# Skip term of the first slab moved from TensorE to VectorE, with a new instruction order on VectorE and a new order of the last output matmuls

## Chip, cores and metric

The kernel runs on one core of a Trainium2 chip. The metric is the device time of one execution in microseconds (us); the median of several runs is compared. Engine names are those of the profile: PE is TensorE, PEld its weight loads, DVE VectorE, ACT ScalarE, POOL GpSimd, SP the queue from which nearly all DMAs are issued.

## What is computed

The input x is 2048 x 512 in bf16. Each row is normalised to xn. From xn come two branches whose product is added to x:

```
xn  = layernorm(x)
Bu  = xn @ B_bar^T                       # complex, 512 states
h_t = Lam_bar * h_(t-1) + Bu_t           # scan over the 2048 rows
s   = 2 * Re(h @ C^T) + xn * Dskip       # Dskip: the skip term
g   = silu((gelu(xn @ w_gate) * (xn @ w_up)) @ w_down)      # inner width 1376
out = x + s * g
```

## The kernel before

The 2048 rows are four slabs (s = 0 to 3) of 512 rows, and a slab is four groups (m = 0 to 3) of 128 rows. All of x stays in SBUF in one tile, `x_tok`, with 16 groups of 512 columns. A slab goes through these steps:

- **Norm.** VectorE (slabs 0 to 2) or ScalarE (`ln_act`, L548, slab 3) sums the statistics; `ln_out` (L573) lets ScalarE write xn, lets a DMA transpose it into `xnT`, and, where `skip` is called, lets VectorE write z = xn * Dskip (L571), so that the skip term can be added later.
- **FFN.** For j = 0 to 10, `ffn` (L451) makes a gate and an up tile of 512 rows x 128 inner columns (`gu_mm`, L223, eight matmuls); ScalarE evicts both (L463, L464), and VectorE multiplies them into `at`, two j at a time (L469; the last, odd one at L467).
- **Scan.** `u_pair` (L365) makes Bu for half of the states (h = 0 or 1), and `chain` (L402) queues VectorE's work on it: rotate in two products (`pp`, `qq`, L391) and two sums into `Wt` (L395), four scans (L421), four tiny carries (L438 to L441), rotate back in the same way into `hst`.
- **Down.** `down` (L471) makes the FFN output of a group with 11 matmuls; ScalarE takes its silu into `g2` (L481).
- **y.** `y_mm` (L484) makes a group's s with eight matmuls from `hst` and C (L491). Where no z exists (slab 0, and groups 2 and 3 of slab 3), four more matmuls of 128x128 against diagonal matrices of Dskip add the skip term on TensorE (L496). `epi` (L503) is VectorE's end: `yt` = y + z where z exists (L512), `yg` = y * g2 (L513), `ot` = yg + x (L514), then the store. `y_halves` (L519) does the last group in two halves.

Around slab s + 1's FFN the y of slab s are made: `Y_AT` (L360) names the four j after which y_mm of group 0 to 3 stands in TensorE's order. After the FFN of a slab stand the two `u_pair` of the next slab and then the four `down`. In the end (L656 to L664) y of group 0 stands ahead of the four `down` of slab 3, and the other three y behind them.

The order on VectorE is set by a small planner when the program is built. `clk` holds a time for PE and for DVE; `dve(ready, cost, f)` (L348) places an instruction now, after it has let waiting ones go that fit ahead of it by their costs, and `later` (L353) puts scan work on the waiting list; `flush` (L340) empties it up to a named chain, which `y_mm` does ahead of its matmuls. The costs are constants in the text (1.15 for a product, 1.19 for a scan, 0.95 or 1.6 for `epi`). On the chip each engine then runs its own list in that order, and waits where a semaphore says so.

At the start x and the gate and up weights are loaded on SP; the weights come in three pieces of columns (`CUTS`, L93). The x of slab 3 is loaded by `load_x(3)` (L633) during slab 0. xn has four buffers, `ot` two, z nine.

Of the kernel before, what the change touches and what calls it, by code (L numbers as in the profile page):

```python
# [11 lines left out]
ALU = mybir.AluOpType  # L12
# [7 lines left out]
def kernel(  # L20
# [69 lines left out]
        nc.sync.dma_start(out=x_tok[:, a:b, :], in_=x_r[:, a:b, :])  # L90
    for i, v in enumerate((A_log_dt, A_Lambda_im, A_Lambda_re, A_Dskip)):
        nc.scalar.dma_start(out=pv[4 * i : 4 * i + 4, :], in_=v.rearrange("(k p) -> k p", p=P))
    CUTS = (0, 3 * P, 8 * P, F)  # L93

    def load_gu(i):
        a, b = CUTS[i], CUTS[i + 1]
        nc.sync.dma_start(out=wg[:, :, a:b], in_=wg_r[:, :, a:b])
        nc.sync.dma_start(out=wu[:, :, a:b], in_=wu_r[:, :, a:b])

    def load_x(s):  # L100
        nc.sync.dma_start(out=x_tok[:, s * M : (s + 1) * M, :], in_=x_r[:, s * M : (s + 1) * M, :])
# [6 lines left out]
    load_gu(0)  # L108
    load_x(1)
    load_gu(1)  # L110
    load_x(2)
    nc.sync.dma_start(out=Db[:], in_=A_Dskip.unsqueeze(0).to_broadcast([P, D]))
    for h in range(2):
        for ri, src in enumerate((A_B_re, A_B_im)):
            for pt in (h * H2, h * H2 + 1):
                nc.sync.dma_start_transpose(
                    out=BT[:, ri, :, pt * P : (pt + 1) * P], in_=src[pt * P : (pt + 1) * P, :]
                )
    load_gu(2)


    warm = work.tile([P, TS], BF16, name="warm", tag="yg")
# [33 lines left out]
    def bn(s, m):  # L156
        nc.vector.bn_stats(out=st[:, s, m, :], in_=x_tok[:, s * M + m, :])
# [41 lines left out]
        else:  # L199
            eng.tensor_copy(out=o, in_=tp[:, k0:k1, :])  # L200

    bn(0, 0)
    bn(0, 1)
    bn_end(0, 0)
    bn_end(0, 1)
    rstd(0, 0, 2)
# [30 lines left out]
    for j in range(SPLIT):  # L237
        for up in range(2):
            early[j, up] = gu_mm(0, j, up, 0, TS // 2)
        if j == 0:  # L240
            tps += [t_xn0(2, xs[2]), t_xn0(3, xs[3])]
            xnT_out(nc.scalar, 3, tps[3])
    STT(out=thn[:], in0=lim, scalar=1.0 / (2.0 * math.pi), in1=dt_[:], op0=ALU.mult, op1=ALU.mult)
    TT(out=a1[:], in0=lre, in1=dt_[:], op=ALU.mult)
    nc.gpsimd.tensor_tensor(out=rho[:], in0=euler[:], in1=a1[:], op=ALU.pow)
# [111 lines left out]
    ini = {}  # L357
    U_BUFS = 3
    U0_AT = (5, 7)
    Y_AT = {1: (5, 7, 9, 10), 2: (1, 2, 3, 4), 3: (2, 4, 6, 8)}  # L360

    def ca_wide():
        ACT(out=v4(ca[:]), in_=ch[:, :, NB : NB + NA].unsqueeze(3).to_broadcast(W4), func=AF.Copy)  # L363
# [19 lines left out]
    def rotate(dst, src, h, ops, ready, key):  # L383
        hs = slice(h * H2, (h + 1) * H2)
        W = [P, 2, H2, TS]
        box = {}

        def mul(key, tab):
            def f():
                box[key] = work.tile(W, BF16, name=key, tag=key, bufs=1)  # L390
                TT(out=box[key][:], in0=src()[:], in1=tab[:, hs, :].unsqueeze(1).to_broadcast(W), op=ALU.mult)  # L391
            return f

        def comb(i, op):
            return lambda: TT(out=dst()[i], in0=box["pp"][:, i, :, :], in1=box["qq"][:, 1 - i, :, :], op=op)  # L395

        later(ready, 1.15, mul("pp", cos_b), key)
        later(ready, 1.15, mul("qq", sin_b), key)
        for i in range(2):
            later(ready, 0.6, comb(i, ops[i]), key)  # L400

    def chain(s, h, U, hst):  # L402
        hs = slice(h * H2, (h + 1) * H2)
        ready = now() + 0.9
        box = {}

        def wt():
            box["W"] = work.tile([P, 2, H2, TS], BF16, name="Wt", tag="Wt", bufs=1)
            return [box["W"][:, i, :, :] for i in range(2)]

        def wt_dst():
            return wt() if "W" not in box else [box["W"][:, i, :, :] for i in range(2)]

        rotate(wt_dst, lambda: U, h, (ALU.add, ALU.subtract), ready, ("u", s, h))

        def scan(q, ri):
            def f():
                if "F" not in box:
                    box["F"] = work.tile([P, 2, H2, TS], BF16, name="Ft", tag="Ft", bufs=1)
                pt = h * H2 + q  # L420
                nc.vector.tensor_tensor_scan(  # L421
                    out=box["F"][:, ri, q, :], data0=rho[:, pt : pt + 1].to_broadcast([P, TS]),
                    data1=box["W"][:, ri, q, :], initial=0.0 if s == 0 else ini[h][:, ri, q : q + 1],
                    op0=ALU.mult, op1=ALU.add,
                )
            return f

        for q in range(H2):
            for ri in range(2):
                later(ready, 1.19, scan(q, ri))  # L430

        def carry():
            fl = box["F"][:, :, :, TS - 1]
            W = [P, 2, H2]
            ta = work.tile(W, FP32, name="ta", tag="ta")
            tb = work.tile(W, FP32, name="tb", tag="tb")
            it = work.tile(W, FP32, name="it", tag=f"it{h}")
            TT(out=ta[:], in0=fl, in1=cS[:, hs].unsqueeze(1).to_broadcast(W), op=ALU.mult)  # L438
            TT(out=tb[:], in0=fl, in1=sS[:, hs].unsqueeze(1).to_broadcast(W), op=ALU.mult)
            TT(out=it[:, 0, :], in0=ta[:, 0, :], in1=tb[:, 1, :], op=ALU.subtract)  # L440
            TT(out=it[:, 1, :], in0=ta[:, 1, :], in1=tb[:, 0, :], op=ALU.add)  # L441
            ini[h] = it

        if s < NS - 1:
            later(ready, 0.5, carry)
        rotate(
            lambda: [hst[:, i, hs, :] for i in range(2)], lambda: box["F"], h, (ALU.subtract, ALU.add), ready,
            ("h", s, h),
        )

    def ffn(s, j, at):  # L451
        fs = min(P, F - j * P)
        if s == 0 and j < SPLIT:
            g_ps, u_ps = (gu_mm(s, j, up, TS // 2, TS, early[j, up]) for up in range(2))
        else:
            g_ps, u_ps = gu_mm(s, j, 0), gu_mm(s, j, 1)
        pe_takes(2 * KT)
        i = j % 2
        if i == 0:
            pair["g"] = work.tile([P, 2, TS], BF16, name="gt", tag="gt", bufs=3)  # L460
            pair["u"] = work.tile([P, 2, TS], BF16, name="ub", tag="ub", bufs=3)
        gt, ub = pair["g"], pair["u"]
        ACT(out=gt[:fs, i, :], in_=g_ps[:fs, :], func=AF.Gelu_apprx_tanh)  # L463
        ACT(out=ub[:fs, i, :], in_=u_ps[:fs, :], func=AF.Copy)  # L464
        lag = 0.9 + (2.5 if s == 0 else 0.5)
        if j == NFT - 1:
            dve(now() + lag, 0.34, lambda: TT(out=at[:fs, j, :], in0=gt[:fs, 0, :], in1=ub[:fs, 0, :], op=ALU.mult))  # L467
        elif i:
            dve(now() + lag, 0.61, lambda: TT(out=at[:, j - 1 : j + 1, :], in0=gt[:], in1=ub[:], op=ALU.mult))  # L469

    def down(s, m, at):  # L471
        m0 = m * P
# [30 lines left out]
    def epi(s, m, y_ps, g2):  # L503
        mg = s * TS + m * P
        yg = work.tile([P, D], BF16, name="yg", tag="yg")
        ot = work.tile([P, D], BF16, name="ot", tag="ot")

        def f():
            y = y_ps
            if (s, m) in zs:  # L510
                y = work.tile([P, D], FP32, name="yt", tag="tt", bufs=3)
                TT(out=y[:], in0=y_ps[:, :], in1=zs[s, m][:], op=ALU.add)  # L512
            TT(out=yg[:], in0=y[:, :], in1=g2[:], op=ALU.mult)  # L513
            TT(out=ot[:], in0=yg[:], in1=x_tok[:, s * M + m, :], op=ALU.add)  # L514

        dve(now() + 0.3, 1.6 if (s, m) in zs else 0.95, f)
        nc.sync.dma_start(out=out_td[mg : mg + P, :], in_=ot[:])

    def y_halves(s, m, hst, g2):  # L519
        m0 = m * P  # L520
        mg = s * TS + m0
        yg = work.tile([P, D], BF16, name="yg", tag="yg")
        ot = work.tile([P, D], BF16, name="ot", tag="ot")
        for i in range(2):
            c = slice(i * D // 2, (i + 1) * D // 2)
            y_ps = psum.tile([P, D // 2], FP32, name="y_ps", tag="ps")
# [40 lines left out]
    zs = {}  # L567

    def skip(s, m, xn):
        zs[s, m] = work.tile([P, D], BF16, name="z", tag="z", bufs=9)  # L570
        dve(now() + 1.5, 0.34, lambda: TT(out=zs[s, m][:], in0=xn[:], in1=Db[:], op=ALU.mult))  # L571

    def ln_out(s, m):  # L573
        xn = work.tile([P, D], BF16, name="xn", tag="xn", bufs=4)
# [4 lines left out]
            skip(s, m, xn)  # L579


    clk["pe"] = 8.1
    clk["dve"] = 10.3
    hsts, ats, g2s = {0: hst0}, {0: at0}, {}


# [15 lines left out]
    dve(10.0, 2.8, lambda: ln_vector(1))  # L602
    ln_vector_small(1)
    dve(13.0, 2.8, lambda: ln_vector(2))
    later(14.0, 1.2, lambda: TT(out=v4(t2_[:]), in0=v4(sa[:]), in1=sB, op=ALU.mult))
    later(14.0, 1.2, lambda: TT(out=v4(t1_[:]), in0=v4(ca[:]), in1=cB, op=ALU.mult))
    later(14.0, 1.2, lambda: TT(out=cos_b[:], in0=t1_[:], in1=t2_[:], op=ALU.subtract))
# [4 lines left out]
    for s in range(NS):  # L612
        for j in range(NFT):
            ffn(s, j, ats[s])
            if s == 0:
# [9 lines left out]
                if j == 2 + M:  # L625
                    load_c(0)
                    nc.sync.dma_start(
                        out=wd[:, 0 : NFT - 1, :],
                        in_=B_w_down[0 : (NFT - 1) * P, :].rearrange("(k p) d -> p k d", p=P),
                    )  # L630
                    nc.sync.dma_start(out=wd[:FL, NFT - 1, :], in_=B_w_down[(NFT - 1) * P : F, :])
                    load_c(1)
                    load_x(3)  # L633
                if j in U0_AT:
                    chain(0, U0_AT.index(j), u_pair(0, U0_AT.index(j)), hst0)
            else:
                if j in Y_AT[s]:
                    m = Y_AT[s].index(j)
                    epi(s - 1, m, y_mm(s - 1, m, hsts[s - 1]), g2s[s - 1, m])
                if s < NS - 1 and 1 <= j < 1 + M:  # L640
                    ln_out(s + 1, j - 1)
        if s < NS - 1:
            hsts[s + 1] = work.tile([P, 2, NPT, TS], BF16, name="hst", tag="hst")
            ats[s + 1] = work.tile([P, NFT, TS], BF16, name="at", tag="at")
# [9 lines left out]
            if s == 1:  # L654
                ln_small(3)
    s = NS - 1  # L656
    y0 = y_mm(s, 0, hsts[s])
    for m in range(M):
        g2s[s, m] = down(s, m, ats[s])
        if m == 0:  # L660
            epi(s, 0, y0, g2s[s, 0])
    for m in range(1, M - 1):
        epi(s, m, y_mm(s, m, hsts[s]), g2s[s, m])
    y_halves(s, M - 1, hsts[s], g2s[s, M - 1])  # L664

# [29 lines left out]
```

## Time and profile before

| what | value |
|---|---|
| time, median of 5 runs | 185.05 us (184.84 to 185.34) |
| time of the profiled execution | 185.34 us |
| its span | 183.5 us, so 1.84 us lie outside it |
| granted TensorE clock | 1.0 |
| PE busy | 177.5 us (97%), 847 matmuls recorded of 863 in the program |
| DVE busy | 163.7 us (89%), 258 instructions |
| ACT busy | 113.0 us (62%) |
| POOL busy | 24.4 us (13%) |
| scans, L421 | 32 of 1272 ns (24 with a carry) |
| z = xn * Dskip, L571 | 10, median 418 ns |
| yt, L512 | 10 of 681 ns |
| diagonal matmuls, L496 and L534 | 20 and 4 |

A row of the timeline has its start, its length (for several instructions from the first start to the last end), engine, line, operation, tiles and count; square brackets hold the idle time of the engine ahead of it and who ended it. Matmuls overlap in a pipeline, so the step from start to start tells their price, not their length. Sixteen of the matmuls left no record; where one is lost, the step from one start to the next is twice as long without any wait.

### The profile page before, as it was taken

Reading aid. Unit: us, or ns where it says so; the run is one execution under the profiler, and the core shown is the slowest. Engines: PE = TensorE matmul, PEld = TensorE weight load, DVE = VectorE, ACT = ScalarE, POOL = GpSimd, SP = SyncE. Lnnn points to the kernel's source line nnn. Section 1 sums busy time; section 2 is a strip of 40 time slices with the busy share of each in tenths; the row PEclk is TensorE's granted clock in tenths of the full one; section 3 lists DMA queues with packets and bytes.
Section 4 is the critical chain, followed back from the end, with each engine's and each line's share of the span. In section 5 each row is a group of like instructions: output and inputs, shape, how many; then the busy total and the mean of one; then the engine's idle time right before and its main releaser. Section 6 shows DMA issues by size and latency. Waiting matters only on the chain.

```text
span 183.5 us, 2436 instructions
## 1 busy us (share of the span) xinstructions
PE 177.5 (97%) x847; PEld 83.9 (46%) x863; DVE 163.7 (89%) x258; ACT 113.0 (62%) x196; POOL 24.4 (13%) x44
## 2 busy tenths in 40 slices
PE   7899999999999999999999999999999999999992
PEld 2474444444444444544444444444444444444452
DVE  4798899999997999999999999999999999996053
ACT  3179997768899954347789665667529444471210
POOL 3569931910000000000003000000000000000000
PEclk9999999999999999999999999999999999999999
DMA  5999484696001310000000032200000010000002
GB/s 147 321 372 140 100 228 86 161 265 172 0 0 27 67 49 32 0 29 29 0 4 0 29 88 57 57 5 0 0 0 0 0 31 24 6 30 29 29 4 86
DMA packets 24588, 12.39 MB, mean 68 GB/s; under 512 B 15776, under 2 KB 24576, under 8 KB 24576
## 3 DMA queue, kind: packets, MB, share of 16 engines
q1 hardware_dynamic: 24400, 12.16, 26.1%
q8 instruction: 7, 0.11, 0.3%
q10 hardware_dynamic: 176, 0.07, 0.1%
q14 instruction: 5, 0.04, 0.1%
HBM read 6.46 MB, written 2.10 MB: 47 GB/s over the span
## 4 chain that ended last, share of the span: by engine, by line
PE 82%; ACT 9%; DVE 5%; issue 1%; DMA 1%; DVEq 0%
PE f_ps L476 21%; PE up_ps L230 16%; PE g_ps L230 16%; PE u_ps L375 13%; PE y_ps L491 13%; PE w_ps L149 3%; ACT gt L463 3%; ACT ub L464 2%; ACT xn L575 2%; DMA out_dram<-ot 1%; DVE hst L395 1%; ACT L463 1%; DVE qq L391 1%; PE y_ps L496 0%; ACT ca L363 0%
## 5 line engine op out<-in xcount | busy, mean ns | idle before, releaser
L230 PE MATMUL g_ps<-xnT,wg 128*128 128x512 bf16 (+2 forms) x181 | 45.3, 370 | 0.6 <-ACT xnT L198 0.5
L230 PE MATMUL up_ps<-xnT,wu 128*128 128x512 bf16 (+2 forms) x181 | 45.0, 370 | 0.1
L463 ACT ACTIVATE gt<-g_ps 128x512 bf16<-128x512 f32 (+1 forms) x44 | 26.9, 612 | 21.1 <-PE g_ps L230 20.8
L476 PE MATMUL f_ps<-wd,at 128*128 128x512 bf16 (+1 forms) x173 | 38.5, 379 | 0.2
L464 ACT ACTIVATE ub<-up_ps 128x512 bf16<-128x512 f32 (+1 forms) x44 | 27.1, 615 | 7.9 <-PE up_ps L230 7.4
L421 DVE TENSOR_TENSOR_SCAN Ft<-rho,it,Wt 128x512 bf16<-128x512 f32 x24 | 29.7, 1272 | 0.0
L491 PE MATMUL y_ps<-C,hst 128*128 128x512 bf16 x115 | 28.1, 379 | 0.5 <-DVE hst L395 0.2
L375 PE MATMUL u_ps<-xnT,BT 128*128 128x512 bf16 x126 | 28.3, 379 | 0.1
L230 PEld LDWEIGHTS <-wu 128*128 128x128 bf16 (+1 forms) x184 | 18.4, 100 | 19.6
L230 PEld LDWEIGHTS <-wg 128*128 128x128 bf16 (+1 forms) x184 | 18.1, 100 | 19.7 <-issue 0.5
L476 PEld LDWEIGHTS <-at 128*128 128x128 bf16 (+1 forms) x176 | 17.2, 98 | 20.9
L380 ACT ACTIVATE U<-u_ps 128x512 bf16<-128x512 f32 x32 | 19.0, 616 | 8.5 <-PE u_ps L375 8.5
L481 ACT ACTIVATE g<-f_ps 128x512 f32<-128x512 f32 x16 | 9.6, 598 | 16.3 <-PE f_ps L476 16.3
L375 PEld LDWEIGHTS <-BT 128*128 128x128 bf16 x128 | 12.5, 98 | 14.8
L491 PEld LDWEIGHTS <-hst 128*128 128x128 bf16 x120 | 11.7, 98 | 14.5 <-DVE hst L395 0.7
L469 DVE TENSOR_TENSOR at<-gt,ub 128x1024 bf16<-128x1024 bf16 x20 | 13.6, 678 | 0.0
L512 DVE TENSOR_TENSOR yt<-y_ps,z 128x512 f32<-128x512 f32 x10 | 6.8, 681 | 7.1 <-PE y_ps L491 7.1
L395 DVE TENSOR_TENSOR hst<-pp,qq 128x1024 bf16<-128x1024 bf16 x16 | 10.6, 688 | 0.2
L395 DVE TENSOR_TENSOR Wt<-pp,qq 128x1024 bf16<-128x1024 bf16 x16 | 10.4, 687 | 0.2
L575 ACT ACTIVATE xn<-x_tok,nb,rs 128x512 bf16<-128x512 bf16 x12 | 10.3, 856 | 0.0
L391 DVE TENSOR_TENSOR pp<-U,cos_b 128x2048 bf16<-128x2048 bf16 x8 | 9.8, 1225 | 0.4
L391 DVE TENSOR_TENSOR pp<-Ft,cos_b 128x2048 bf16<-128x2048 bf16 x8 | 9.8, 1220 | 0.1
(109 smaller groups left out, 159.0 us busy)
## 6 DMA issues: line engine op xcount, KB each, us to landing
out_dram<-ot SPq DMA_DIRECT2D x15, 128.0 KB, 1.7
x_tok<-in_A_x_dram SPq DMA_DIRECT2D x3, 512.0 KB, 6.2
wd<-in_B_w_down_dram SPq DMA_DIRECT2D x1, 1280.0 KB
wg<-in_B_w_gate_dram SPq DMA_DIRECT2D x1, 640.0 KB
wu<-in_B_w_up_dram SPq DMA_DIRECT2D x1, 640.0 KB, 8.5
wg<-in_B_w_gate_dram SPq DMA_DIRECT2D x1, 384.0 KB, 3.7
wu<-in_B_w_up_dram SPq DMA_DIRECT2D x1, 384.0 KB
wg<-in_B_w_gate_dram SPq DMA_DIRECT2D x1, 352.0 KB
```

The costliest lines, as they stand in the source:

```text
L230: nc.tensor.matmul(ps[:fs, a:b], lhsT=w[:, kt, fsl], rhs=xnT[:, kt, s * TS + a : s * TS + b], start=(kt == 0), stop=(kt == KT - 1),)
L375: nc.tensor.matmul(u_ps[:, :], lhsT=BT[:, ri, kt, pt * P : (pt + 1) * P], rhs=xnT[:, kt, cols], start=(kt == 0), stop=(kt == KT - 1),)
L380: ACT(out=U[:, ri, q, :], in_=u_ps[:, :], func=AF.Copy)
L391: TT(out=box[key][:], in0=src()[:], in1=tab[:, hs, :].unsqueeze(1).to_broadcast(W), op=ALU.mult)
L395: return lambda: TT(out=dst()[i], in0=box["pp"][:, i, :, :], in1=box["qq"][:, 1 - i, :, :], op=op)
L421: nc.vector.tensor_tensor_scan(out=box["F"][:, ri, q, :], data0=rho[:, pt : pt + 1].to_broadcast([P, TS]), data1=box["W"][:, ri, q, :], in ...
L463: ACT(out=gt[:fs, i, :], in_=g_ps[:fs, :], func=AF.Gelu_apprx_tanh)
L464: ACT(out=ub[:fs, i, :], in_=u_ps[:fs, :], func=AF.Copy)
L469: dve(now() + lag, 0.61, lambda: TT(out=at[:, j - 1 : j + 1, :], in0=gt[:], in1=ub[:], op=ALU.mult))
L476: nc.tensor.matmul(f_ps[:, :], lhsT=at[:fs, k, m0 : m0 + P], rhs=wd[:fs, k, :], start=(k == 0), stop=(k == NFT - 1))
L491: nc.tensor.matmul(y_ps[:, :], lhsT=hst[:, j // NPT, j % NPT, m0 : m0 + P], rhs=C2[:, j // NPT, j % NPT, :], start=(j == 0), stop=((s, m) ...
L575: ACT(out=xn[:], in_=x_tok[:, s * M + m, :], func=AF.Identity, scale=rs[:, s, m : m + 1], bias=nb[:, s, m : m + 1])
```

## The change

- The skip term of slab 0 is also made on VectorE. Its z are written into the part of `x_tok` that belongs to slab 3, and `load_x(3)` moves from slab 0 to behind the last y of slab 0, which reads them.
- Slab 0's y therefore lose their diagonal matmuls and their `epi` gets the `yt` step.
- The planner's costs are changed, and with them the order on VectorE; the y of slab 0 stand after j = 7, 8, 9, 10 (were 5, 7, 9, 10), those of slab 1 after j = 2, 3, 4, 5 (were 1 to 4), and the `ln_out` of slab 3 begin one j later (`XN_AT`).
- The y of group 0 of slab 3 stands behind the four `down`, so all four y of slab 3 stand together at the end.
- The gate and up weights come in four pieces, and one more piece stands ahead of the x of slab 2. `ot` has three buffers.

```
-    CUTS = (0, 3 * P, 8 * P, F)
+    CUTS = (0, 2 * P, 5 * P, 8 * P, F)
...
     load_gu(1)
+    load_gu(2)
     load_x(2)
...
-    load_gu(2)
+    load_gu(3)
...
-    Y_AT = {1: (5, 7, 9, 10), 2: (1, 2, 3, 4), 3: (2, 4, 6, 8)}
+    Y_AT = {1: (7, 8, 9, 10), 2: (2, 3, 4, 5), 3: (2, 4, 6, 8)}
+    XN_AT = {1: 1, 2: 2}
...
-        later(ready, 1.15, mul("pp", cos_b), key)
-        later(ready, 1.15, mul("qq", sin_b), key)
+        later(ready, 1.17, mul("pp", cos_b), key)
+        later(ready, 1.19, mul("qq", sin_b), key)
         for i in range(2):
-            later(ready, 0.6, comb(i, ops[i]), key)
+            later(ready, 0.62, comb(i, ops[i]), key)
...
-                later(ready, 1.19, scan(q, ri))
+                later(ready, 1.215, scan(q, ri))
...
-        ot = work.tile([P, D], BF16, name="ot", tag="ot")
+        ot = work.tile([P, D], BF16, name="ot", tag="ot", bufs=3)
...
-        dve(now() + 0.3, 1.6 if (s, m) in zs else 0.95, f)
+        dve(now() + 0.3, 1.75 if (s, m) in zs else 1.07, f)
...
-        zs[s, m] = work.tile([P, D], BF16, name="z", tag="z", bufs=9)
-        dve(now() + 1.5, 0.34, lambda: TT(out=zs[s, m][:], in0=xn[:], in1=Db[:], op=ALU.mult))
+        if s == 0:
+            z = x_tok[:, (NS - 1) * M + m, :]
+        else:
+            z = work.tile([P, D], BF16, name="z", tag="z", bufs=9)[:]
+        zs[s, m] = z
+        dve(now() + 1.5, 0.36, lambda: TT(out=z, in0=xn[:], in1=Db[:], op=ALU.mult))
...
-    clk["pe"] = 8.1
-    clk["dve"] = 10.3
+    clk["pe"] = 8.3
+    clk["dve"] = 10.6
...
     dve(13.0, 2.8, lambda: ln_vector(2))
+    for m in range(M):
+        skip(0, m, xs[m])
...
                     load_c(1)
-                    load_x(3)
...
-                if s < NS - 1 and 1 <= j < 1 + M:
-                    ln_out(s + 1, j - 1)
+                if s < NS - 1 and XN_AT[s] <= j < XN_AT[s] + M:
+                    ln_out(s + 1, j - XN_AT[s])
+        if s == 1:
+            load_x(3)
...
-    y0 = y_mm(s, 0, hsts[s])
     for m in range(M):
         g2s[s, m] = down(s, m, ats[s])
-        if m == 0:
-            epi(s, 0, y0, g2s[s, 0])
-    for m in range(1, M - 1):
+    for m in range(M - 1):
         epi(s, m, y_mm(s, m, hsts[s]), g2s[s, m])
     y_halves(s, M - 1, hsts[s], g2s[s, M - 1])
```

The planner's costs of the two `at` products rise too, from 0.34 to 0.36 and from 0.61 to 0.63.

More of the change, by code (lines that the diff above doesn't have):

```diff
@@ L200, in xnT_out @@
             eng.tensor_copy(out=o, in_=tp[:, k0:k1, :])
-    bn(0, 0)
-    bn(0, 1)
+    for m in range(2):
+        bn(0, m)
     bn_end(0, 0)
@@ L239 @@
             early[j, up] = gu_mm(0, j, up, 0, TS // 2)
-        if j == 0:
-            tps += [t_xn0(2, xs[2]), t_xn0(3, xs[3])]
-            xnT_out(nc.scalar, 3, tps[3])
+            if j == 0 and up == 1:
+                tps += [t_xn0(2, xs[2]), t_xn0(3, xs[3])]
+                xnT_out(nc.scalar, 3, tps[3])
     STT(out=thn[:], in0=lim, scalar=1.0 / (2.0 * math.pi), in1=dt_[:], op0=ALU.mult, op1=ALU.mult)
@@ L466, in ffn @@
         if j == NFT - 1:
-            dve(now() + lag, 0.34, lambda: TT(out=at[:fs, j, :], in0=gt[:fs, 0, :], in1=ub[:fs, 0, :], op=ALU.mult))
+            dve(now() + lag, 0.36, lambda: TT(out=at[:fs, j, :], in0=gt[:fs, 0, :], in1=ub[:fs, 0, :], op=ALU.mult))
         elif i:
-            dve(now() + lag, 0.61, lambda: TT(out=at[:, j - 1 : j + 1, :], in0=gt[:], in1=ub[:], op=ALU.mult))
+            dve(now() + lag, 0.63, lambda: TT(out=at[:, j - 1 : j + 1, :], in0=gt[:], in1=ub[:], op=ALU.mult))
     def down(s, m, at):
@@ L511, in f @@
                 y = work.tile([P, D], FP32, name="yt", tag="tt", bufs=3)
-                TT(out=y[:], in0=y_ps[:, :], in1=zs[s, m][:], op=ALU.add)
+                TT(out=y[:], in0=y_ps[:, :], in1=zs[s, m], op=ALU.add)
             TT(out=yg[:], in0=y[:, :], in1=g2[:], op=ALU.mult)
             TT(out=ot[:], in0=yg[:], in1=x_tok[:, s * M + m, :], op=ALU.add)
-        dve(now() + 0.3, 1.6 if (s, m) in zs else 0.95, f)
+        dve(now() + 0.3, 1.75 if (s, m) in zs else 1.07, f)
         nc.sync.dma_start(out=out_td[mg : mg + P, :], in_=ot[:])
@@ L522, in y_halves @@
         yg = work.tile([P, D], BF16, name="yg", tag="yg")
-        ot = work.tile([P, D], BF16, name="ot", tag="ot")
+        ot = work.tile([P, D], BF16, name="ot", tag="ot", bufs=3)
         for i in range(2):
```

## Prediction

> **What bounds the kernel.** I read the page first: which engine has no idle time.
>
> ```profile
> PE 177.5 (97%) x847; PEld 83.9 (46%) x863; DVE 163.7 (89%) x258; ACT 113.0 (62%) x196; POOL 24.4 (13%) x44
> PE 82%; ACT 9%; DVE 5%; issue 1%; DMA 1%; DVEq 0%
> ```
>
> PE is the bound, and DVE is close behind. I then went along PE's matmuls from start to start. From 8.3 us to the last start at 180.0 a 128x512 matmul follows every 0.216 us, almost without a break. The doubled steps that recur every 10.8 us are the 16 lost records. One true wait is left, in the timeline of PE at the first y of slab 0:
>
> ```profile
> 61.74 1.46 PE L491 MATMUL y_ps<-C,hst 128*128 128x512 bf16 x6
> 63.36 0.61 PE L491 MATMUL y_ps<-C,hst 128*128 128x512 bf16 x2 [0.16 <-DVE hst L395]
> 63.80 0.39 PE L496 MATMUL y_ps<-diagI,xnT 128*128 128x128 bf16 x4
> 64.02 0.38 PE L230 MATMUL g_ps<-xnT,wg 128*128 128x512 bf16 x1
> ```
>
> The seventh matmul was due at 61.74 + 6 x 0.216 = 63.04 and came at 63.36: 0.32 us lost to DVE's second `hst` (the bracket shows only 0.16, since it counts from the end of the pipelined matmul before). The last two rows give the price of the diagonal matmuls: four of them from 63.80 to 64.02, 0.056 each.
>
> So the time is PE's list, plus what DVE makes PE wait, plus the tail. A change can win only by shortening PE's list or that wait, and it loses wherever DVE comes later than PE.
>
> **Removed from PE.** Slab 0's y lose 4 x 4 diagonal matmuls: 16 x 0.056 = 0.89 us. The Trainium skill (TensorE: Matmul & The Clock Gate, Back-to-back issue gap) says that in a stream of weight load and matmul pairs one with 128 columns costs about 81 ns, since weight loads count too, and that the isolated 56 ns is too low. By it the gain is 16 x 0.081 = 1.30 us. The row is for this very stream, and the next g_ps matmul follows it without a gap; I take 0.89.
>
> The wait of 0.32 goes too, if `hst` is in time for the moved y. Slab 1's j = 0 begins at 61.74 - 6 x 1.727 = 51.38 (one j is eight matmuls, 1.727), so with y behind j = 7 its seventh matmul is due at 51.38 + 8 x 1.727 + 1.29 = 66.49. VectorE's new order puts ahead of that `hst`: z of slab 2's last group, then qq, hst, at, hst. That z waits for ScalarE's xn:
>
> ```profile
> 61.91 0.88 ACT L575 ACTIVATE xn<-x_tok,nb,rs 128x512 bf16<-128x512 bf16 x1
> ```
>
> It ends at 62.79, so z starts at 62.82 and, with the steps of the DVE rows (z 0.33, qq 1.25, hst 0.60, at 0.60, hst 0.69), the second `hst` is there at 66.30, PE sees it 0.06 later: 0.13 us in hand. What is late next is not this y but the next slab's.
>
> **Added to DVE.** Four z for slab 0 (L571, step 0.33 each, 1.34 us) in the first 20 us, and four `yt` (L512, 0.72 from start to start where `yg` waits for it, 2.87 us) between 67 and 81. The z have cover: DVE's waits before 63 us. Before, z waited 2.2 us for xn (waits table), x of slab 2 another 0.67; adding the rows up in the new order leaves some 2.2 us of such waits between 15 and 63, and after each of them DVE is back on ScalarE's time. The `yt` have no cover: from that z on, DVE never waits until slab 1's second `hst`. This is the stretch before:
>
> ```profile
> 62.80:95.10 32.30, 31.98 (x158) 15.05 (x160) 31.78 (x47) 18.81 (x36) 0.00 (x0) 1.00 0.08 22
> ```
>
> (32.30 us; PE, PEld, DVE, ACT busy). DVE is busy 31.78 of it, and its rows show where it starts and ends:
>
> ```profile
> 63.22 0.42 DVE L571 TENSOR_TENSOR z<-xn,Db 128x512 bf16<-128x512 bf16 x1
> 63.55 1.22 DVE L391 TENSOR_TENSOR pp<-U,cos_b 128x2048 bf16<-128x2048 bf16 x1
> ...
> 93.64 1.29 DVE L395 TENSOR_TENSOR hst<-pp,qq 128x1024 bf16<-128x1024 bf16 x2
> ```
>
> From behind z (63.55) to the end of that `hst` (94.93) it took 31.38 us. In the new order the same stretch holds in addition: the qq and two hst of slab 0, which stood ahead of this z (1.25 + 0.60 + 0.72 = 2.57), four yt (2.87), and the four small steps of `ln_small`, now ahead of slab 1's rotation (0.54, from the rows of L557 to L560). Sum 37.36 us. It starts behind the z at 62.82 + 0.33 = 63.15, so the first of slab 1's last two `hst` is there at 99.91 and the second at 100.51.
>
> PE wants them here:
>
> ```profile
> 94.93 1.03 PE L230 MATMUL g_ps<-xnT,wg 128*128 128x512 bf16 x4
> ...
> 98.38 1.89 PE L491 MATMUL y_ps<-C,hst 128*128 128x512 bf16 x8
> ```
>
> Before, slab 2's FFN starts at 94.93 and y at 98.38, 3.5 us behind the finished `hst` (94.93): room that the `yt` now use up. After, PE is there at 94.93 - 0.89 - 0.32 = 93.72; y stands one j later, behind three j, at 98.90. Its third matmul (the first that reads the second half of the states) is due at 99.33 and can start at 99.91 + 0.06 = 99.97: a new wait of 0.64 us. The seventh is then due at 100.84 and finds its `hst` (100.57). So what is taken from PE is mostly given back at this place. Queued behind the wait on PE is everything.
>
> **Later stages.** Work is the same, the order differs. In slab 3 no y covers the last `at` any more: `down` starts straight behind the FFN, and needs the last `at` at its 11th matmul, 2.16 us later. After up's end ScalarE takes some 0.7 (L464), and DVE's order has at, one scan of 1.27, then this `at` (0.41); added up in order it is there about 0.5 us early. The second half of `hst` of slab 3, needed in the old order at 163.2, is now needed behind the four `down` (9.5 us later) and comes over 1.5 us early. I count nothing for both; if DVE lags by more, their price is one for one.
>
> **The tail.** Four y now follow each other, 1.73 us each on PE. An `epi` with z has taken 1.79 (158.92 to 160.71) to 2.03 us (176.31 to 178.34), so DVE falls 0.1 to 0.4 behind, which the third y, whose `epi` is only 1.06, gives back. The last half was bound like this:
>
> ```profile
> 180.28 0.42 DVE L538 TENSOR_TENSOR yg<-y_ps,g 128x256 bf16<-128x256 f32 x1
> 180.74 0.29 DVE L539 TENSOR_TENSOR ot<-yg,x_tok 128x256 bf16<-128x256 bf16 x1
> ```
>
> DVE's end (181.03) lies 0.83 behind PE's (180.20); in the new order it comes out at 0.79 to 0.95. I count 0. The third `ot` buffer ends a wait of 0.25 for a store, inside this same tail.
>
> **Loads.** Two more DMAs stand ahead of x of slab 2. The Trainium skill (DMA: Bandwidth & Descriptors, Anatomy of one DMA and Bandwidth) speaks against cutting: a fixed 2 us a DMA, and pieces of at least 1 MiB. By it two more cost 4 us. The trace's packet records say less: loads overlap, a 1280-byte packet takes 55 ns and a 768-byte one 36; the same bytes need 1024 x 27 + 2048 x 36 ns instead of 1024 x 36 + 1024 x 55 over 16 engines, 0.4 us more (27 ns is the 512-byte packet). x of slab 2 lands near 14.8 instead of 14.3, under the 2.2 us cover. The DMAs behind (transposes of B, later w_down) are issued 1 to 2.5 us later; B's are needed 3.5 us, w_down 2.5 us after they landed. I take 0, ends 0 and the 4 us of the page. The x of slab 3 is issued after slab 0's last `ot`, at some 81; alone it needs about 3.5 us (an estimate: 512 packets of 46 ns over 16 engines and the 1.7 us of a store), 6.2 in the crowded start; ScalarE wants it at 87.7. Nothing either way.
>
> **Sum.** -0.89 - 0.32 + 0.64 + 0 = -0.57 us. The span of 183.5 becomes 182.9, the profiled 185.34 becomes 184.8; against the median 185.05 the forecast is 184.5.
>
> **Rivals.**
> - *DVE keeps up* (0.13): DVE reaches the stretch earlier or `hst` comes 0.6 earlier. For it: half a per cent of 37 us is 0.2. Against: z hangs on ScalarE's xn, and nothing in between waits. No new wait: -1.21, 183.8 us.
> - *The cut loads cost the page's price* (0.09). x of slab 2 lands 4 us late; DVE's statistics stand first in its queue, and all of slab 0's DVE work behind them. 2.2 of it are covered, and about 1.4 to 1.8 come out at slab 0's and slab 1's first y: 185.05 - 0.57 + 1.6 = 186. It turns to a loss once x of slab 2 is over 2.2 + 0.6 = 2.8 us late. Against: the packet records.
> - *A second wait* (0.12): the last `at` of slab 3, or slab 0's `hst` with its 0.13 in hand, are 0.5 late: the gain is gone, 185.0.
> - That the change doesn't do what it says: PE's list has 16 fewer matmuls, so no.
>
> **Chances.** The likeliest case (0.66), with the new wait between 0.35 and 0.95, spans 184.2 to 184.8. With the no-wait case and the second wait I give 183.8 to 185.0. A difference under 0.2% (0.37 us) is what a measurement of this kernel can't tell from none. Faster by more, under 184.68: most of the first case and the no-wait case, 0.73; same 0.17; slower 0.10.
>
> **What would show it.** PE idle at y of slab 1's group 0 near 99.3, released by DVE's hst, for 0.4 to 0.9 us, and no idle at 63; the four `yt` between 67 and 81 with no DVE wait from 63 to 100. Wrong if that idle is missing (faster), if x of slab 2 lands after 17 us, or if f_ps of slab 3 waits for `at`.

## The result and the profile after

The changed kernel takes 184.48 us (median of 42 runs, 184.08 to 185.03); the kernel before took 184.83 us (median of 79 runs, 184.40 to 185.55) beside it. The ratio is 0.9982, 95% interval 0.9976 to 0.9988: 0.35 us faster, between 0.22 and 0.44. The forecast was a gain of 0.57 us. So the sign is right. That the predicted time of 184.5 is met as well is luck: the kernel before came out 0.2 us faster than in its first five runs, and the gain is only some 60% of the forecast. At 0.18% it falls just inside the band of 0.2% that the prediction called "same".

The profiled execution of the changed kernel took 184.47 us with a span of 182.7 us and a granted TensorE clock of 0.998. First the busy times of the page, and its chain of work by engine:

```profile
PE 175.7 (96%) x831; PEld 82.7 (45%) x847; DVE 168.0 (92%) x266; ACT 112.5 (62%) x196; POOL 18.6 (10%) x44
PE 60%; DVE 21%; ACT 8%; SPq 4%; DMA 4%; issue 1%
```

PE lost 16 recorded matmuls and 1.8 us of busy time, DVE gained eight instructions (four z, four `yt`) and 4.3 us. In the chain, DVE rose from 5% to 21%: the chain now runs through DVE for a long stretch. Where it leaves DVE is seen in PE's timeline. First at slab 0's first y, where the old wait was, then at slab 1's first y:

```profile
64.67 1.89 PE L493 MATMUL y_ps<-C,hst 128*128 128x512 bf16 x8
```

```profile
98.36 0.59 PE L493 MATMUL y_ps<-C,hst 128*128 128x512 bf16 x2
99.52 1.47 PE L493 MATMUL y_ps<-C,hst 128*128 128x512 bf16 x5 [0.56 <-DVE hst L397]
100.83 1.03 PE L231 MATMUL g_ps<-xnT,wg 128*128 128x512 bf16 x4
```

At 64.67 eight matmuls run through: the wait of 0.32 us is gone. At 98.36 two matmuls start; the third was due at 98.36 + 2 x 0.216 = 98.79 and starts at 99.52: a new wait of 0.73 us, ended by DVE's `hst`. (From 99.52 to the next gate matmul at 100.83 there are six steps of 0.216: one of the eight matmuls left no record.) DVE's own timeline shows why the `hst` comes then:

```profile
62.30 0.43 DVE L578 TENSOR_TENSOR z<-xn,Db 128x512 bf16<-128x512 bf16 x1 [0.44 <-ACT xn L582]
62.65 1.22 DVE L393 TENSOR_TENSOR qq<-Ft,sin_b 128x2048 bf16<-128x2048 bf16 x1
...
65.11 0.68 DVE L397 TENSOR_TENSOR hst<-pp,qq 128x1024 bf16<-128x1024 bf16 x1
...
68.71 0.69 DVE L514 TENSOR_TENSOR yt<-y_ps,x_tok 128x512 f32<-128x512 f32 x1
69.43 0.69 DVE L515 TENSOR_TENSOR yg<-yt,g 128x512 bf16<-128x512 f32 x1
...
98.77 1.29 DVE L397 TENSOR_TENSOR hst<-pp,qq 128x1024 bf16<-128x1024 bf16 x2
```

z waits for ScalarE's xn (the bracket), and behind it, from 62.65 to 98.77 + 1.29 = 100.06, lie 37.41 us without a wait of DVE. The busy times of this stretch tell the same: DVE's instructions fill 36.73 of the 37.41 us, and the rest are gaps of at most 0.04 us between them.

```profile
62.65:100.06 37.41, 36.69 (x169) 16.72 (x170) 36.73 (x57) 24.73 (x49) 2.09 (x2) 1.00 0.11 32
```

(us; busy us of PE, PEld, DVE, ACT, POOL with their counts; granted clock; DMA share; GB/s.)

To see the whole, I cut each profiled execution into three parts: *start*, up to the first gate matmul; *body*, from there to the start of PE's last matmul; *end*, from there to the end of the span.

| kernel | start | body | end | span |
|---|---|---|---|---|
| before | 8.29 | 171.69 | 3.50 | 183.47 |
| changed | 7.71 | 171.27 | 3.71 | 182.68 |
| changed, profiled again (e12) | 7.65 | 171.20 | 3.68 | 182.53 |

The body is 0.42 to 0.49 shorter, the end 0.18 to 0.21 longer. The start differs from execution to execution: it lies between 7.52 and 8.37 us in the five profiles with three pieces of weights and between 7.49 and 8.11 in the nine with four. That is why the spans of two profiles can't be compared directly, and why I compare body and end, and the medians. Body and end together: 175.19 before, 174.98 and 174.88 changed, so -0.21 and -0.31, beside -0.35 in the medians. What is left for the start is at most 0.14 us, within what the medians can tell.

### The profile page after: what moved, and what is told of

It is laid out like the page before. It is cut to its first block, busy times and chain, and to the rows that moved or that the text cites. A ratio compares the mean times of both kernels' runs of the same rounds, so it can differ in the third digit from the quotient of the medians.

```text
span 182.7 us, 2411 instructions
## 1 busy us (share of the span) xinstructions
PE 175.7 (96%) x831; PEld 82.7 (45%) x847; DVE 168.0 (92%) x266; ACT 112.5 (62%) x196; POOL 18.6 (10%) x44
## 4 chain that ended last, share of the span: by engine, by line
PE 60%; DVE 21%; ACT 8%; SPq 4%; DMA 4%; issue 1%
PE f_ps L478 16%; PE up_ps L231 12%; PE g_ps L231 12%; PE y_ps L493 10%; PE u_ps L377 9%; DVE Ft L423 5%; DMA x_tok<-in_A_x_dram 4%; DVE qq L393 3%; ACT xn L582 3%; DVE pp L393 3%; ACT ub L466 2%; ACT gt L465 2%; SPq L98 2%; DVE hst L397 2%; DVE yg L515 2%; DVE Wt L397 1%
## 5 line engine op out<-in xcount | busy, mean ns | idle before, releaser
L231 PE MATMUL up_ps<-xnT,wu 128*128 128x512 bf16 (+2 forms) x184 | 45.5, 370 | 0.2
L231 PE MATMUL g_ps<-xnT,wg 128*128 128x512 bf16 (+2 forms) x178 | 44.8, 369 | 0.8 <-ACT xnT L199 0.5
L158 DVE BATCH_NORM_STATS2 st<-x_tok 128x6 f32<-128x512 bf16 x12 | 7.5, 682 | 4.3 <-DMA x_tok<-in_A_x_dram 4.3
L515 DVE TENSOR_TENSOR yg<-yt,g 128x512 bf16<-128x512 f32 x14 | 9.7, 693 | 0.6
```

The costliest lines, as they stand in the source:

```text
L231: nc.tensor.matmul(ps[:fs, a:b], lhsT=w[:, kt, fsl], rhs=xnT[:, kt, s * TS + a : s * TS + b], start=(kt == 0), stop=(kt == KT - 1),)
```

## The experiments

The theory (**T**) is that of the prediction: PE's list became 0.89 us shorter and the old wait went, but DVE's longer stretch makes a new wait at slab 1's first y that takes most of it back. The rivals at this point: that the four pieces of weights cost something in the crowded start (**L**), and that the new order at the end costs something (**E**). The runs are named e1 to e12 in the order they were made; they are told by subject. Every ratio is to the kernel before, run beside it on the same chip.

### e1: slab 1's y one j later

```
-    Y_AT = {1: (7, 8, 9, 10), 2: (2, 3, 4, 5), 3: (2, 4, 6, 8)}
+    Y_AT = {1: (7, 8, 9, 10), 2: (3, 4, 5, 6), 3: (2, 4, 6, 8)}
```

> The changed kernel with slab 1's y one more j later (behind j = 3, 4, 5, 6 instead of 2, 3, 4, 5). Wait theory: the new wait of TensorE for VectorE's hst at 98.6 to 99.5 (0.73 us) is all that the gain has lost; y is now due 1.73 us later and finds its hst, so TensorE's last start comes 0.73 earlier than in the changed kernel, 1.2 us under the kernel before less what the start and the stores vary (time 183.6 to 183.9 where the kernel before has 184.8). Rival, the loads: the gain is short because the weights were cut into more pieces; then moving y changes nothing and the time stays at 184.5. Rival, shifted debt: VectorE, never idle here, hands the lag on to the next y, and another wait of 0.4 or more appears in slab 2.

Measured: 183.58 us, ratio 0.9934 (0.9920 to 0.9948); body 170.47. PE's timeline at the same place:

```profile
99.15 1.03 PE L231 MATMUL up_ps<-xnT,wu 128*128 128x512 bf16 x3
100.01 1.89 PE L493 MATMUL y_ps<-C,hst 128*128 128x512 bf16 x8
101.74 1.03 PE L231 MATMUL g_ps<-xnT,wg 128*128 128x512 bf16 x4
```

The y starts 1.65 later and its eight matmuls run through. The wait of 0.73 is gone and the body is 0.80 shorter (0.73 beside e12's). No other wait of PE comes in its place. T holds: this one wait held back most of the change's gain.

### e2: slab 0's skip back on TensorE, the rest kept

```
-    for m in range(M):
-        skip(0, m, xs[m])
```

> The changed kernel without slab 0's z: its skip term is made on TensorE again by 16 diagonal matmuls, all else kept. Wait theory: +0.89 for TensorE's list, and the four yt (2.87 us) leave VectorE, so the wait at slab 1's first y (0.73) is gone: +0.16 there. But the planner gives another order, and adding up rows in it shows the last at of slab 3 some 0.5 us late for the first down behind it: together +0.6 to +0.8 over the changed kernel, 0.2 to 0.5 over the kernel before. Loads theory: only the 0.89 comes back, +0.9 over the changed kernel, and the wait at slab 1's y stays.

Measured: 185.29 us, ratio 1.0030 (1.0014 to 1.0047); body 171.79, that is +0.52 on the changed kernel. There is no wait at 99 us. There is another in slab 3's `down`:

```profile
162.15 2.32 PE L478 MATMUL f_ps<-wd,at 128*128 128x512 bf16 x9
164.67 1.69 PE L478 MATMUL f_ps<-wd,at 96*128 96x512 bf16 x7 [0.20 <-DVE at L469]
```

Ten matmuls precede the eleventh, which was due at 162.15 + 10 x 0.216 = 164.31 (one of the ten left no record) and came at 164.67: 0.36 us for the last `at`. The sum closes: +0.89 (sixteen diagonal matmuls again) - 0.73 + 0.36 = +0.52. With the 81 ns of the page that the prediction weighed, it would have been 1.30 - 0.73 + 0.36 = 0.93; so 0.056 is the price in this stream. The new order alone, without the z, does not win. And the wait at the last `at`, which the prediction held as a rival, exists in this order; with the z of slab 0 in place it does not arise.

### e3: the suspected cost doubled

One `yt` of slab 0 is computed twice with the same values (the output is unchanged), 0.72 us more on DVE inside the stretch:

```
-                TT(out=y[:], in0=y_ps[:, :], in1=zs[s, m], op=ALU.add)
+                for _ in range(2 if (s, m) == (0, 1) else 1):
+                    TT(out=y[:], in0=y_ps[:, :], in1=zs[s, m], op=ALU.add)
```

> The changed kernel with the yt addition of slab 0's group 1 made twice (same values): one more VectorE step of 0.72 us at about 72 us. Wait theory: nothing between 62 and 100 us absorbs it, so the wait at slab 1's first y grows from 0.73 to 1.45 and the time by 0.7 us over the changed kernel, 0.35 over the kernel before. Loads theory, or a VectorE that has room: no change.

Measured: 184.97 us, ratio 1.0011 (1.0000 to 1.0022); body 171.98, +0.71.

```profile
98.16 0.59 PE L493 MATMUL y_ps<-C,hst 128*128 128x512 bf16 x2
100.03 1.47 PE L493 MATMUL y_ps<-C,hst 128*128 128x512 bf16 x5 [1.27 <-DVE hst L397]
```

The third matmul was due at 98.16 + 0.43 = 98.59 and came at 100.03: 1.44. So 0.72 us on DVE made the wait 0.71 longer and the body 0.71 longer: one for one, with no slack anywhere in the 37 us.

### e10: only three z of slab 0

```
-    for m in range(M):
+    for m in range(1, M):
         skip(0, m, xs[m])
```

> The changed kernel with slab 0's z for three groups only: group 0 keeps its four diagonal matmuls. One yt less (0.72 us) for VectorE, 0.22 more for TensorE. Wait theory: the wait at slab 1's first y falls from 0.73 to 0.1 or 0.2, so TensorE's list is 0.3 us shorter than the changed kernel's in spite of the 0.22 (184.2 where the changed kernel has 184.5). Theory that each diagonal matmul saved is won: 0.22 slower, 184.7.

Measured: 184.14 us, ratio 0.9954 (0.9937 to 0.9970); body 170.68. The y of slab 1:

```profile
98.92 1.89 PE L493 MATMUL y_ps<-C,hst 128*128 128x512 bf16 x7
100.65 1.03 PE L231 MATMUL g_ps<-xnT,wg 128*128 128x512 bf16 x4
```

From 98.92 to 100.65 are eight steps of 0.216: no wait. The expectation had left 0.1 to 0.2 of it, but PE itself also comes 0.22 later here. One `yt` less (0.72) takes away the 0.73 of wait and costs four diagonal matmuls (0.22): 171.27 - 0.73 + 0.22 = 170.76, measured 170.68. Doing less of the change wins more, since the fourth `yt` takes 0.72 us of DVE to save 0.22 us of PE, and DVE had no room for it.

### e4, e5, e6: weights in three pieces again, and what that stands for

e4 goes back to the three pieces:

```
-    CUTS = (0, 2 * P, 5 * P, 8 * P, F)
+    CUTS = (0, 3 * P, 8 * P, F)
...
-    load_gu(2)
     load_x(2)
...
-    load_gu(3)
+    load_gu(2)
```

> The changed kernel with the gate and up weights in the old three pieces. Wait theory: x of slab 2 lands about 0.5 to 1 us earlier and the transposes of B are issued 1 to 2 us earlier, all under cover; the wait at slab 1's y stays 0.7 and the time stays within 0.2 us of the changed kernel. Loads theory: faster than the changed kernel by 0.3 us or more.

Measured: 184.16 us, ratio 0.9966 (0.9956 to 0.9977), somewhat better than the changed kernel. L seems to hold, but the table by parts says otherwise: the body is 171.25 (changed: 171.27), and the gain lies in the end, 3.47 instead of 3.71. Three pieces of weights at 10 us can't shorten the last 3 us by their bytes. What they change as well is the number of DMAs. DVE, for its part, ended 1.05 us after PE's last start before and 1.01 after. What stands behind the last store differs. The waits of SP, before and after, at the program's last line (us in total, times, longest):

```profile
SPq L690 <- DMA out_dram<-ot: 1.6, 3, 0.7
```

```profile
SPq L697 <- DMA out_dram<-ot: 2.0, 1, 2.0
```

The last store lands at 182.63 before, and 0.09 us later SP is through with its waits; after the change it lands at 181.59, and SP is through 0.32 later. In the traces SP goes at its end through the DMA semaphores (the counters that tell it of a landing) in a fixed list of six waits, some 0.06 us each, and the DMAs take eight semaphores in turn. Before, the last store has the semaphore that stands last in the list, and SP waits three times, each time for the next store. After, with two more DMAs in the program, the last store has one that stands second: SP sits there 2.0 us, and must still go through the rest when the store has landed. From that landing to the end of the span are 0.84 us before and 1.09 after. If this is it, only the count of DMAs matters, in turns of eight. So two more kernels: e5 keeps four pieces and splits `load_x(3)` in seven (six more: eight more than before in all), e6 keeps three pieces, as in e4, and splits it in three (two more, as in the changed kernel).

```
-            load_x(3)
+            for g in range(M):
+                for c in ((0, D // 2), (D // 2, D)) if g < 3 else ((0, D),):
+                    nc.sync.dma_start(out=x_tok[:, 3 * M + g, c[0] : c[1]], in_=x_r[:, 3 * M + g, c[0] : c[1]])
```

> The changed kernel, with the x of slab 3 loaded in seven pieces instead of one (issued at 81 us, needed at 87, SP idle there). The weights stay in four pieces. End theory: the stores take eight semaphores in turn, and SP's last waits go through them in a fixed list of six pairs; with two more DMAs than before the last store is on the second of the list, so after its landing SP still has four waits to go through (0.06 us each, 0.2 to 0.25 us), which the kernel before does not have. Six more DMAs bring the last store to the end of the list again: 0.2 to 0.3 us faster than the changed kernel, 184.2 where the kernel before has 184.8, with the early loads untouched. Early-load theory (the pieces of the weights themselves cost the 0.3): no change, 184.5.

```
...
-            load_x(3)
+            for a, b in ((12, 13), (13, 14), (14, 16)):
+                nc.sync.dma_start(out=x_tok[:, a:b, :], in_=x_r[:, a:b, :])
```

> The weights in the old three pieces, but the x of slab 3 in three, so that the number of DMAs is that of the changed kernel and the last store is on the second semaphore of the list again. End theory: the 0.3 us that three pieces won are lost again, 184.5. Early-load theory: stays at 184.2.

| kernel | pieces | DMAs against before | body | end | median us | ratio (95%) |
|---|---|---|---|---|---|---|
| changed (e12, beside e9 and e10) | 4 | +2 | 171.20 | 3.68 | 184.39 | 0.9976 (0.9961 to 0.9991) |
| e4 | 3 | 0 | 171.25 | 3.47 | 184.16 | 0.9966 (0.9956 to 0.9977) |
| e5 | 4 | +8 | 171.24 | 3.47 | 184.12 | 0.9962 (0.9949 to 0.9976) |
| e6 | 3 | +2 | 171.18 | 3.68 | 184.30 | 0.9979 (0.9964 to 0.9993) |

And the wait of SP in e5:

```profile
SPq L699 <- DMA out_dram<-ot: 1.8, 3, 0.8
```

With eight more DMAs SP waits three times again, as before; the end is 3.47. With three pieces and two more DMAs, it is 3.68. So L falls, and the end goes with the count: 0.21 us between these four profiles. In all fourteen profiles the last store's landing is followed by 0.84 or 0.85 us where its semaphore stands last (six profiles) and by 1.06 to 1.09 where it stands second (eight). The medians go the same way, by 0.1 to 0.3; their intervals overlap, so it is the end column that tells them apart. E falls with it: e4 and e5 keep the new order of the last y, and their end of 3.47 is no longer than the 3.50 before.

### e8: the old order of the last y, with everything else new

```
+    y0 = y_mm(s, 0, hsts[s])
...
+        if m == 0:
+            epi(s, 0, y0, g2s[s, 0])
-    for m in range(M - 1):
+    for m in range(1, M - 1):
```

> The changed kernel with the old end: y of slab 3's group 0 ahead of the four down. If the new order of the last y is free of charge and no more than that, the time stays within 0.3 us. Theory of the order: the planner has put three scans and the rotation of the last chain behind the last at; rows added up in order give that hst only some 8 us after the FFN, under the cover of the four down. With y ahead of them TensorE stands for some 7 to 8 us: 7 or more us slower than the changed kernel.

Measured: 194.4 us, ratio 1.0523 (1.0500 to 1.0545); body 181.97, +10.7. PE's timeline, and the page's row of the granted clock in 40 slices, with two stretches of it:

```profile
161.84 0.59 PE L493 MATMUL y_ps<-C,hst 128*128 128x512 bf16 x2
170.12 1.46 PE L493 MATMUL y_ps<-C,hst 128*128 128x512 bf16 x3 [7.68 <-DVE hst L397]
```

```profile
PEclk9999999999999999999999999999999999657999
```

```profile
170.20:175.00 4.80, 4.80 (x12) 1.70 (x13) 1.15 (x2) 0.00 (x0) 0.00 (x0) 0.50 0.00 0
175.00:185.00 10.00, 10.00 (x45) 4.37 (x44) 1.12 (x2) 2.39 (x4) 0.00 (x0) 0.94 0.04 13
```

The third matmul was due at 162.28 and came at 170.12: 7.84 us. In DVE's new order the `hst` of slab 3 comes that late, and needs the four `down` (9.5 us) as cover; so putting the four y together at the end isn't an extra of the change but what its DVE order rests on. The wait also cost more than its length: the granted clock fell to 0.50 at 165.86, in the middle of the wait (the row's 6 is the slice from 164.2 to 169.0), and came back at 176.10, when PE had been at work again for 6.0 us (the second stretch still has a mean of 0.94). These 6.0 us at half speed cost 3.0; 7.84 + 3.0 = 10.8, where the body grew by 10.7. The smaller waits, 1.44 us at most, left the clock at 1. The Trainium skill (TensorE: Matmul & The Clock Gate, Part 1: The HAM clock gate) has the clock halve behind an idle window of about 3.4 us. This one trace fits: the clock fell 3.8 us after PE's last matmul had started (162.06). Whether a wait of 2 or 3 us would do it, no run here shows.

### e9: the kernel before, with slab 0's y moved alone

```
-    Y_AT = {1: (5, 7, 9, 10), 2: (1, 2, 3, 4), 3: (2, 4, 6, 8)}
+    Y_AT = {1: (7, 8, 9, 10), 2: (1, 2, 3, 4), 3: (2, 4, 6, 8)}
```

> One part alone, in the kernel before: slab 0's y behind j = 7, 8, 9, 10 instead of 5, 7, 9, 10. Prediction's step: the wait of 0.32 us at 63 us goes, nothing else does; TensorE's list from its first gate matmul to its last start gets 0.3 shorter (171.7 to 171.4), the time 0.2 to 0.3 us (184.6). If that wait only moves to another y, no change.

Measured: 184.48 us, ratio 0.9982 (0.9966 to 0.9999). PE has no wait at slab 0's first y any more:

```profile
65.35 1.89 PE L491 MATMUL y_ps<-C,hst 128*128 128x512 bf16 x8
```

The body of its profile is 172.28, longer than before's 171.69, but a wait at the start is in it that this edit didn't make:

```profile
7.52 0.70 PE L230 MATMUL g_ps<-xnT,wg 128*128 128x256 bf16 x4 [0.47 <-ACT xnT L198]
9.16 0.61 PE L230 MATMUL up_ps<-xnT,wu 128*128 128x256 bf16 x4 [0.94 <-DMA wu<-in_B_w_up_dram]
```

Here PE began at 7.52, and the up weights had not landed: the up matmuls start 1.64 us behind the gate's first, where in the profile of before (8.29 and 8.83) it was 0.54. So 1.10 us are lost to weights that landed late in this execution; e4, with the same three pieces and a start of 7.60, has no such wait. On the other hand PE does not wait here for 0.17 us near 10.8, as it did before. The sum closes: 171.69 - 0.32 + 1.10 - 0.17 = 172.30, measured 172.28; the medians say -0.33. So the move of slab 0's y by itself wins back the old wait, and that is about all that the whole change gains.

### e7, e11, e12: two cures together, and the changed kernel once more

e7 joins e1 with the three pieces of e4; e11 joins it with the seven DMAs of e5. e12 is the changed kernel unedited.

> The two edits together that made the changed kernel faster: slab 1's y behind j = 3, 4, 5, 6 and the weights in three pieces. Wait theory with end theory: both add, since one lies in TensorE's list and the other behind the last store: 0.73 + 0.25 under the changed kernel, 1.3 to 1.5 us under the kernel before (183.3 to 183.5 where it has 184.8). If the gain of three pieces was early and under the same wait, no more than the 183.6 of later y alone.

> The changed kernel with slab 1's y one j later and the x of slab 3 in seven pieces (the last store on the last semaphore of the list), weights in four pieces. Wait theory with end theory: TensorE's list 170.5 us from its first gate matmul to its last start, 3.5 us from there to the end; 1.4 us under the kernel before, 183.4 to 183.6, and the fastest of all together with the one that has later y and three pieces.

> The changed kernel once more, unedited, beside these. The stretch from the first gate matmul to TensorE's last start should repeat to 0.1 us (171.3), and that from there to the end too (3.7). What varies from one execution to the next should be the start alone, when the first gate matmul comes (7.5 to 8.4 us in the profiles so far); the time 0.2 to 0.5 us under the kernel before.

| kernel | start | body | end | body + end | median us (runs) | ratio (95%) |
|---|---|---|---|---|---|---|
| e1 | 7.69 | 170.47 | 3.68 | 174.15 | 183.58 (6) | 0.9934 (0.9920 to 0.9948) |
| e7 | 8.37 | 170.47 | 3.47 | 173.94 | 183.67 (6) | 0.9937 (0.9917 to 0.9956) |
| e11 | 7.57 | 170.53 | 3.46 | 173.99 | 183.76 (6) | 0.9935 (0.9913 to 0.9957) |
| e12 | 7.65 | 171.20 | 3.68 | 174.88 | 184.39 (12) | 0.9976 (0.9961 to 0.9991) |

In the profiles the two cures add up (0.73 and 0.21). The expectation that e7 and e11 would be 0.2 us faster than e1 does not show in the medians of six runs each: the 0.2 us is less than their spread (0.23 to 0.9 us). All three beat both kernels, by 1.05 to 1.25 us against the kernel before that ran beside each.

## Why the prediction was right, and what it mis-sized

**Diagonal matmuls, -0.89: right.** e2 gives them back and its sum closes to 0.01 with 0.056 each; the 0.081 of the page would have left 0.4 unexplained.

**The old wait, -0.32: right.** The y at 64.67 runs through: its `hst` ends at 65.80, and the seventh matmul is due at 64.67 + 6 x 0.216 = 65.97, so of the 0.13 us in hand 0.11 were there (with the 0.06 until PE sees it). e9 removes this wait alone.

**The new wait, +0.64: right in place and cause, measured 0.73 (0.70 in e12).** The prediction let DVE's stretch end its first `hst` 36.76 us behind z and had the third matmul due 36.18 behind it; measured, the `hst` is there 36.81 behind z (99.46 - 62.65) and the matmul was due at 36.14. Five hundredths from DVE, four from PE. The start of everything 0.5 us earlier (62.65 instead of 63.15) is the start of this execution and drops out of the difference. e1, e3 and e10 remove, double and remove it, each with the body following by 0.6 to 0.8.

**The tail, 0: wrong, +0.21.** This is the one term that failed: "I count 0" looked at DVE's end behind PE's, and there it is right (1.05 before, 1.01 after). But the span doesn't end with DVE; what follows waits until SP has gone through its list of semaphores. Two DMAs more moved the last store from the last place of that list to the second. The prediction did count the two DMAs, at the place where they load, and found nothing there; what they cost lies at the other end of the program. The third `ot` buffer did end its wait of 0.25 for a store, but DVE came out no earlier against PE.

**Loads, 0: right.** x of slab 2 landed later, but not by the 4 us of that rival. (The 4 us were an estimate of the prediction's own: the page that it names gives its fixed 2 us for DMAs issued from GpSimd, not from SP, and does not say that they add up for DMAs that overlap.)

```profile
15.37 2.47 DVE L158 BATCH_NORM_STATS2 st<-x_tok 128x6 f32<-128x512 bf16 x4 [2.26 <-DMA x_tok<-in_A_x_dram]
```

It is there at 15.37 (estimated 14.8, before 14.3). But one pair of executions is not enough here: over all profiles DVE begins with it at 14.30 to 15.45 with three pieces (median 14.38 of five) and at 14.62 to 15.58 with four (median 14.88 of nine). So 0.5 us later is the fair figure, and the estimate was good. The body shows nothing of it: e4 and e5, three pieces and four, have the same body to 0.01. The chain of the changed profile runs through this load, but the new wait doesn't hang on it: in the six profiles that have this wait at its size in the changed kernel, the load is there between 14.34 and 15.37, and the third matmul comes 91.7 to 91.8 us behind the first gate matmul in each. x of slab 3 left no wait either. Two small sums of this part were off without weight: the packets give 0.5 us, not 0.4, and x of slab 3 comes to 3.2 us, not 3.5.

**The last `at` and slab 3's `hst`, 0: right.** Neither has a wait in the changed kernel. e2 (0.36) and e8 (7.84) show that both do wait in another order.

**The sum.** -0.89 - 0.32 + 0.73 + 0.21 = -0.27, against -0.21 and -0.31 in the two profiles and -0.35 (0.22 to 0.44) in the medians. The profile's -0.21 has 0.06 more in it from the third group of gate matmuls near 10.2 us, where PE waited 0.23 instead of 0.17; in e12, with smaller waits at both places, the same sum gives -0.30. So the forecast of -0.57 missed 0.30: 0.21 in the tail, 0.09 in the size of the wait. Of the rivals, "DVE keeps up" needed 0.7 us that DVE did not have, "the cut loads cost the page's price" is ruled out by the body of e4 and e5, and "a second wait" did not occur.

**What stays open.** Why the start lies anywhere between 7.5 and 8.4 us was not tried; it is larger than nearly all the differences here and is likely the main part of the spread between runs, but that is argued, not shown. The wait of 1.10 us for the up weights in e9 was seen in one of five profiles with three pieces and in none of nine with four; whether smaller first pieces spare some executions such a wait, and so add to the gain in the medians, was not tested.

## What to carry to other kernels

When work moves from the bounding engine to one that is nearly as busy, add up the second engine's list from its last wait to the next place where the first needs its result: here the 0.89 us saved on PE cost 2.87 us of uncovered work on DVE, and one wait at the end of DVE's 37 us took back 0.73. Then look at when that result is asked for: asking one j later (e1) was worth more than the change itself, and moving slab 0's y alone (e9) gained as much as the whole. And compare two profiles part by part, start, body and end, since a difference of 0.3 us in the whole can be three of them with both signs.

## What the runs showed of the hardware that was not expected

- The end of this program depends on how many DMAs it has issued (tried with 0, 2 and 8 more): 3.46 to 3.52 us from PE's last start to the end of the span where the last store's semaphore stands last in SP's final list, 3.68 to 3.76 where it stands second.
- A wait of 7.84 us on PE cost 10.7 us: the granted clock fell to 0.50 after 3.8 us and stayed there for 6.0 us of work behind the wait. Waits up to 1.44 us cost their own length.
- Two more DMAs ahead of x of slab 2 let SP issue it at 7.6 to 8.7 us instead of 4.9 to 6.0, yet it was there only some 0.5 us later (medians of nine and five profiles).
